# Value tiles copied by an engine where they keep their partitions, turned tiles copied by VectorE, and late loads moved behind the weights

## The chip, the cores and the metric

The kernel runs on one core of a Trainium2 chip. The metric is device time in microseconds of one execution. A core has five engines with a queue of instructions each, worked off in order: TensorE (PE; its weight loads are listed apart, as PEld), VectorE (DVE), ScalarE (ACT), GpSimd (POOL) and SyncE (SP). SP only issues DMAs here; GpSimd also issues some.

## The reference

Two branches run over the same x (2048 rows of 576) and are mixed by a gate per row.

```python
def _A_ref(x, mem0, Wq, Wk, Wv, Wo, seg_len):       # 32 heads of 128, 8 memory rows, segments of 32
    mask = (idx[:, None] < M) | (idx[:, None] >= idx[None, :])
    for s in range(n_seg):                          # 64 segments, one after the other
        h = concatenate([mem, x[:, 32*s:32*s+32]])  # 40 rows
        q, k, v = h @ Wq, h @ Wk, h @ Wv            # 576 -> 32 x 128 each
        p = softmax(where(mask, q k^T * scale, -1e9))
        o = (p v) @ Wo
        mem = o[:, :8]                              # feeds the next segment
        outs.append(o[:, 8:])
def _B_ref(x, wqkv, wo):                            # full attention, 32 heads of 18, 2048 x 2048
    ...
g = sigmoid((x * gate_w).sum(-1))
return g * a + (1 - g) * b
```

Branch A is a recurrence: a segment can't start before the memory rows of the one before are known. Branch B has no such order and is used to fill the time between A's steps.

## The kernel before, in words

**A planner writes the order.** Every piece of work is an `Op` with the engines that may do it, an assumed duration on each, the pieces that it needs and a priority from the table `RANK`. `Plan.run` (L104) places them one by one on simulated engines: `choose` (L197) takes, for each engine, the piece that can start first, then the one of the lowest priority number. Tokens stand for buffers and PSUM banks: a piece that takes one waits until another gives it back. SP's transfers get an assumed landing time (`transfer`, L65). The instructions of each engine are then emitted in this order. If TensorE would stand still in the plan while an accumulator of branch B is open, a filler matmul on zeros is inserted ("warm"; L767 in the column form of four matmuls, L773 in the full form of one).

**Start (some 120 us).** x is turned and projected to branch B's q, k and v, which are stored to DRAM (L622 to L664). At the same time GpSimd issues the loads of A's weights (L537, L542: four pieces each of wv, wq, wk), each one behind a mark that VectorE writes. `carrier(n, far)` names the queue of a load: SP, or GpSimd where `far` is true. Key chunks (`load_k`, L716) go to GpSimd from chunk 3 on, value chunks (`load_v`, L745) from chunk 4, query chunks (`load_q`) from chunk 2.

**Branch B's visits.** 512 visits: four row-tiled matmuls for scores (L795), one ScalarE exponential over 128x2048 (L804), four column-tiled matmuls with the values (L813). `ahead` and `behind` in `RANK` spread them over the segments.

**Branch A's segment.** The 40 rows are 32 rows computed in the recurrence (8 memory rows and 24 of x) and 8 rows of x that are projected beforehand, which are put in later. The 32 rows are projected in six blocks Q0, K0, Q1, K1, V0, V1 (L1120, 20 matmuls each; four column groups of the array hold four groups of heads). Each block is evicted from PSUM by VectorE or ScalarE into a tile `tm` of 128x512 (L412 or L410), of which there are four. Q and K tiles are turned by a DMA transpose (L1178, on SP) into `tt`, and copied into the tile `qk` (L1187) by VectorE or GpSimd. A V tile holds its rows in four blocks of 32 partitions; they have to be in `v_sb` at partitions 0 to 31 and 64 to 95, so four DMAs of SP carry each V tile there:

```python
for j in range(4):
    o = hf * 1024 + (j % 2) * 512
    dma(out=opened["v_sb"][64 * (j // 2):64 * (j // 2) + CT, o:o + 512], in_=tm[32 * j:32 * j + CT, :])
```

Blocks 0 and 2 keep their partitions in this, blocks 1 and 3 move down by 32. Then, for each half `hf` of the heads: scores (`psh`, L1203), exponential (L1213, ScalarE), masking by a minimum (`mn`, L1219, VectorE), sums (`pss`, L1229), reciprocal (L1238, VectorE), its broadcast (`prb`, L1246), the product (`nm`, L1256, VectorE), the product with v (`pso`, L1267), its eviction into `ot` (`co`, L412 or L410) and the output projection (`acc`, L1034). The memory rows are folded back (L1314) into the next segment's input. `pso` needs the transfers of v and the normalised weights. GpSimd also copies x columns into the next input (L1071 to L1073), the early projected rows into `qk` (L1089) and rows of `ot` aside (L1366).

SP's queue in a segment is: four transposes, eight v transfers, the early projected rows of a later segment, two loads of the early projected v rows (L1098).

Of the kernel before, what the change touches and what calls it, by code (L numbers as in the profile page):

```python
# [14 lines left out]


RANK = {
    "switch": 0.563, "near": 0, "early": 0.353, "wait": 0.266, "Q0": 0.487, "K0": 1.599, "Q1": 3.227,
    "K1": 2.483, "V0": 3.547, "V1": 5.796, "t0": 1.149, "t1": 0.73, "ph0": 6.746, "ph1": 0.999, "sm0": 1.555,
    "sm1": 0.05, "bc0": 0.05, "bc1": 1.126, "po0": 0.191, "po1": 0.05, "op0": 7.959, "op1": 0.124,  # L20
    "fo": 0.288, "lo0": 6.529, "lo1": 1.982, "la": 3.0, "ob": 0.777, "eQ": 5.514, "eK": 1.557, "eV": 0.427,
    "co": 0.869, "le": 4.086, "xp": 8.668, "mn": 0.05, "ct": 2.895, "fin": 16.977, "la_gate": 1, "lo_gate": 1,
    "ahead": 56, "behind": 1, "tail": 0.458, "gap": 0, "cool": 12.71,
}


# [18 lines left out]
class Plan:  # L45
# [56 lines left out]
        return end + self.DRAIN[dep.eng]  # L102

    def run(self):  # L104
        free = {e: 0.0 for e in ("PE", "DVE", "ACT", "POOL", "SP")}
        waiting = {e: [] for e in free}
        mode = None
        for op in self.ops:
            op.left = len(op.deps)
            for d in op.deps:  # L110
                d.users.append(op)
        for op in self.ops:
            if op.left == 0:
                for e in op.engs:
                    waiting[e].append(op)
        order = []
        n = len(self.ops)
        extra = 0
        open_ = False
        recent = []  # L120
        best = {}
        dirty = set(free)
        while len(order) < n + extra:
            for e in dirty:
                best[e] = self.choose(e, waiting[e], free[e], mode)
            pick = None
            for e in free:
                b = best[e]
                if b is not None and (pick is None or b[0] < best[pick][0]):
                    pick = e  # L130
            if pick is None:
                stuck = [(o.name, o.take) for e in free for o in waiting[e]]
                raise RuntimeError(f"nothing can be placed: {stuck[:20]}")
            est, op = best[pick]
            if pick == "PE" and open_ and self.warm is not None:
                for m in ("col", "full"):
                    if m not in (mode, op.mode):
                        continue
                    turn = 0.0 if mode == m else self.SWITCH
                    done = sum(d for t, d in recent if t > free["PE"] - 2.5)  # L140
                    if est - free["PE"] < self.WARM + turn + RANK["gap"] or done > RANK["cool"]:
                        continue
                    w = Op("warm", "PE", self.WARM, self.warm[m], [], 9.0, m, (), (), 0.0)
                    w.dmas, w.kb, w.slots, w.left = 0, 0.0, {}, 0
                    w.eng, w.start, w.end = "PE", free["PE"], free["PE"] + self.WARM + turn
                    free["PE"], mode = w.end, m
                    recent.append((w.end, self.WARM))
                    order.append(w)
                    extra += 1
                    pick = None  # L150
                    break
                if pick is None:
                    dirty = {"PE"}
                    continue
            waiting_engs = op.engs
            for e in waiting_engs:
                waiting[e].remove(op)
            dirty = set(waiting_engs)
            dirty.add(pick)
            dur = op.dur[op.engs.index(pick)]  # L160
            op.eng, op.start = pick, est
            if pick == "PE":
                if op.mode != mode:
                    dur += self.SWITCH
                mode = op.mode
                if op in self.opens:
                    open_ = True
                if op in self.closes:
                    open_ = False
                recent = recent[-8:]  # L170
                recent.append((est, dur * self.ARRAY[mode]))
            op.end = est + dur
            free[pick] = op.end
            if op.dmas and pick == "POOL":
                op.tail = 2.2 + op.kb / 250.0
            elif op.dmas:
                self.transfer(op)
                dirty.add("SP")
            for t in op.take:
                held = self.tokens[t]  # L180
                got = max(x for x in held if x[0] <= est + 1e-9)
                held.remove(got)
                op.slots.setdefault(t, []).append(got[1])
                dirty |= set(free)
            for t, taker, k in op.give:
                self.tokens[t].append((op.end + op.tail + self.DRAIN[pick], taker.slots[t][k]))
                dirty |= set(free)
            order.append(op)
            for u in op.users:
                u.left -= 1  # L190
                if u.left == 0:
                    for e in u.engs:
                        waiting[e].append(u)
                        dirty.add(e)
        return order

    def choose(self, e, ops, now, mode):  # L197
        found = []
        for op in ops:
            est = now  # L200
            for d in op.deps:
                a = self.after(d, e)
                if a > est:
                    est = a
            if op.dmas and e != "POOL":
                step = op.dur[op.engs.index(e)] / op.dmas
                for j in range(min(op.dmas, self.LANES)):
                    est = max(est, self.lanes[j] - j * step)
            blocked = False
            for t in set(op.take):  # L210
                k = op.take.count(t)
                held = sorted(self.tokens[t])
                if len(held) < k:
                    blocked = True
                    break
                if held[k - 1][0] > est:
                    est = held[k - 1][0]
            if not blocked:
                found.append((est, op))
        if not found:  # L220
# [32 lines left out]
def kernel(  # L253
# [475 lines left out]
    def load_k(c):  # L729
        g, kc = divmod(c, NQC)  # L730
        use = visits.get(("kuse", c - NKR))


        def fn(e):
            by_head(ktd, g, slice(kc * QC, (kc + 1) * QC), kring[c % NKR], False, queue(e))

        k_of[c] = add(f"lk{c}", *carrier(4, c >= 3), fn, [use, z_k[c % NKR], *stores_for(1, g, [kc])], prio=0.6, dmas=4, kb=90)

    def load_v(c):
        g, kc = divmod(c, NQC)  # L740
# [7 lines left out]
            )  # L748

        deps = [v_stores[hf * NKB + kb] for kb in range(4 * kc, 4 * kc + 4)]  # L750
        v_of[c] = add(f"lv{c}", *carrier(1, c >= 4), fn, [use, *deps], prio=0.65, dmas=1, kb=128)

    def load_q(i):
        g, qc = divmod(i, NQC)
        use = visits.get(("quse", i - NQR))

        def fn(e):
            by_head(qtd, g, slice(qc * QC, (qc + 1) * QC), qring[i % NQR], False, queue(e))

        q_of[i] = add(f"lq{i}", *carrier(4, i >= 2), fn, [use, z_q[i % NQR], *stores_for(0, g, [qc])], prio=0.55, dmas=4, kb=90)  # L760

    fin_state = {}
    last_vi = last_va = None
# [288 lines left out]
    for s in range(n_seg):  # L1052
# [100 lines left out]

        def put_v(hf, s=s):
            def fn(e):
                tm = box["tm", s, 2, hf]
                for j in range(4):
                    o = hf * 1024 + (j % 2) * 512
                    dma(  # L1159
                        out=opened["v_sb"][64 * (j // 2):64 * (j // 2) + CT, o:o + 512],  # L1160
                        in_=tm[32 * j:32 * j + CT, :],
                    )
            return fn

        pv0 = add(f"qv0.{s}", "SP", 2.5, put_v(0), [ev0, prev.get("pso0")], prio=0.2, give=(("tm", ev0, 0),), dmas=4, kb=128)
        pv1 = add(f"qv1.{s}", "SP", 2.5, put_v(1), [ev1, prev.get("pso1")], prio=0.2, give=(("tm", ev1, 0),), dmas=4, kb=128)

        acc_state = {}
        ots = []
        mids = {}  # L1170
        for hf in range(2):
            eq, ek, pvx = ((eq0, ek0, pv0), (eq1, ek1, pv1))[hf]

            turned = []
            for a, ev_a in ((0, eq), (1, ek)):
# [9 lines left out]
                def ct(e, hf=hf, s=s, a=a):  # L1185
# [4 lines left out]
                    )  # L1190

                turned.append(add(
                    f"ct{a}{hf}.{s}", ("DVE", "POOL"), (0.36, 0.85), ct, [t_, prev.get(f"psh{hf}")],
                    prio=RANK["ct"], give=(("tt", t_, 0),),
                ))

# [73 lines left out]
                            rhs=et[rr, r * L:(r + 1) * L], start=True, stop=True, tile_position=(64 * jj, 0),  # L1270
                        )

            o_ = add(f"po{hf}.{s}", "PE", 0.34, pso, [n_, lv, pvx], prio=RANK[f"po{hf}"], mode="tall", take=("pb", "pb"))
            cur[f"pso{hf}"] = o_
            for jj in range(2):
                def co(e, hf=hf, s=s, jj=jj):
# [269 lines left out]
```

## Time and profile before

| | |
|---|---|
| time, median of 3 runs | 1522.55 us (1519.33 to 1526.65) |
| span of the profiled execution | 1514.9 us |
| TensorE busy | 1404.0 us, 93% |
| ScalarE busy | 1051.5 us, 69% |
| VectorE busy | 753.8 us, 50% |
| GpSimd busy | 574.6 us, 38% |
| exponential of a visit, L804 | 512 of 1877 ns |
| eviction of a block by VectorE, L412 tm | 382 of 691 ns |
| turned copy, L1187 | 197 on VectorE of 323 ns, 59 on GpSimd of 625 ns |
| v transfers, L1159 | 512 on SP, 32 KB each |
| folds, L1314 | first at 178.6 us, sixteenth at 492.1 us: 20.9 us for a segment |

A line of a group of instructions names the line of code, the engine, the operation, output and input; then how many, their busy time and mean, and how long the engine stood idle ahead of them with what ended that. In an answer on waits a line has the engine, the line that waited, what released it, the total in us, how often and the longest. In a timeline a line has start and duration in us, and in brackets the idle time before it. "issue" stands for time in which the engine waited for nothing that the profile shows.

### The profile page before, as it was taken

The page shows a single profiled execution, that of the slowest core. Times are in us where ns is not written, and L with a number is a line of the kernel's source. Part 1 is how long each engine was busy: PE and PEld are TensorE (multiplying, and loading weights), DVE is VectorE, ACT ScalarE, POOL GpSimd, SP SyncE. Part 2 cuts the span into 40 slices and gives each one's busy share as a digit, 9 for nine tenths or more (in the row PEclk, how much of TensorE's full clock was granted, in tenths as well). Part 3 has the DMA queues.
Part 4 walks back from the last instruction along what each step waited for, and adds up shares of the span by engine and source line. Part 5 has one row for each costly group of instructions (what it writes and reads, how often), then busy time and mean ns, then how long its engine had stood idle before and what let it go on. Part 6 is the DMA issues. An engine that isn't in the chain of part 4 may idle for free.

```text
span 1514.9 us, 69086 instructions
## 1 busy us (share of the span) xinstructions
PE 1404.0 (93%) x30585; PEld 767.0 (51%) x30585; DVE 753.8 (50%) x1735; ACT 1051.5 (69%) x765; POOL 574.6 (38%) x1207
## 2 busy tenths in 40 slices
PE   6789899999999999999999999999999999999997
PEld 4346445555555545554555544555555455454545
DVE  6345454554555544555545554545554444444445
ACT  2125677777778777777778777767777777777770
POOL 6322125433352425343453325333453324333235
PEclk9799999999999999999999999999999999999999
DMA  8776633423333324333334333333334333333234
GB/s 277 225 276 187 132 67 80 84 63 70 68 79 71 67 64 86 73 67 69 72 83 66 68 68 83 72 59 70 79 81 84 60 60 74 60 61 60 51 108 132
DMA packets 355690, 138.52 MB, mean 91 GB/s; under 512 B 301095, under 2 KB 341431, under 8 KB 355391
## 3 DMA queue, kind: packets, MB, share of 16 engines
q1 hardware_dynamic: 327023, 89.55, 28.2%
q0 software_dynamic: 27216, 43.38, 10.0%
q8 instruction: 239, 3.92, 1.1%
q10 hardware_dynamic: 1152, 1.18, 0.3%
q14 instruction: 60, 0.49, 0.1%
HBM read 52.74 MB, written 30.86 MB: 55 GB/s over the span
## 4 chain that ended last, share of the span: by engine, by line
PE 63%; DMA 13%; ACT 12%; SPq 4%; issue 3%; DVE 3%; POOL 2%; ACTq 0%; DVEq 0%; POOLq 0%
PE pvv L1120 25%; ACT etb L804 11%; PE sb L795 10%; PE acc L1034 8%; PE ob L813 7%; DMA v_sb<-tm 5%; SPq L1159 3%; PE pv L894 3%; DMA tt<-tm 2%; PE pq L602 2%; PE ob L767 2%; PE pv L890 2%; DMA vgd<-vt 2%; PE psh L1203 1%; PE pso L1267 1%
## 5 line engine op out<-in xcount | busy, mean ns | idle before, releaser
L804 ACT ACTIVATE etb<-sb 128x2048 bf16<-128x2048 f32 x512 | 961.0, 1877 | 356.0 <-PE sb L795 334.7
L412 DVE CAST tm<-pvv 128x512 bf16<-128x512 f32 x382 | 263.7, 691 | 297.9 <-PE pvv L1120 297.1
L1120 PEld LDWEIGHTS <-ht 128*32 128x32 bf16 x7680 | 204.7, 97 | 187.3 <-DVE ht L1322 11.5
L795 PE MATMUL sb<-qch,kch 32*128 32x512 bf16 x2048 | 205.2, 388 | 33.4 <-ACT etb L804 23.6
L813 PE MATMUL ob<-etb,vch 128*32 128x512 bf16 x2048 | 206.2, 393 | 0.1
L1034 PE MATMUL acc<-wo,ot 128*32 128x144 bf16 x8192 | 161.6, 228 | 10.0 <-issue 9.3
L1034 PEld LDWEIGHTS <-ot 128*32 128x32 bf16 x8192 | 137.2, 98 | 29.9 <-issue 16.7
L1187 POOL COPY qk<-tt 128x512 bf16<-128x512 bf16 x59 | 36.8, 625 | 279.2 <-DMA tt<-tm 279.1
L795 PEld LDWEIGHTS <-kch 32*128 32x128 bf16 x2048 | 65.8, 91 | 151.1 <-issue 124.9
L1120 PE MATMUL pvv<-wq_m,ht 128*32 128x512 bf16 x2048 | 139.6, 380 | 0.3 <-issue 0.3
L1120 PE MATMUL pvv<-wv_m,ht 128*32 128x512 bf16 x2048 | 138.5, 379 | 0.0
L1120 PE MATMUL pvv<-wk_m,ht 128*32 128x512 bf16 x2048 | 135.3, 379 | 0.1
L412 DVE CAST ot<-pso 128x320 bf16<-128x320 f32 x179 | 83.4, 484 | 87.2 <-PE pso L1267 86.9
L813 PEld LDWEIGHTS <-vch 128*32 128x32 bf16 x2048 | 53.0, 93 | 106.6 <-issue 105.2
L1187 DVE COPY qk<-tt 128x512 bf16<-128x512 bf16 x197 | 63.6, 323 | 36.3 <-DMA tt<-tm 35.6
L1089 POOL COPY qk<-xl 128x256 bf16<-128x256 bf16 x128 | 50.4, 403 | 81.2 <-PE psh L1203 70.4
L1071 POOL COPY ht<-xg 128x96 bf16<-128x96 bf16 x64 | 17.1, 267 | 168.4 <-PE pvv L1120 149.7
L716 POOL DMA_DIRECT2D qch<-qtd x120 | 61.0, 515 | 42.6 <-PE sb L795 39.0
L1366 POOL COPY otl<-ot 128x256 bf16<-128x256 bf16 x64 | 25.7, 401 | 135.3 <-DVE ot L412 86.2
L1256 DVE TENSOR_TENSOR et<-et,prb 128x320 bf16<-128x320 bf16 x128 | 61.3, 479 | 31.6 <-PE prb L1246 30.4
L716 POOL DMA_DIRECT2D kch<-ktd x116 | 58.9, 514 | 45.1 <-PE sb L795 22.2
L716 POOL DMA_DIRECT2D otd<-stage x124 | 62.3, 509 | 36.0 <-DVE stage L856 34.9
(148 smaller groups left out, 1892.2 us busy)
## 6 DMA issues: line engine op xcount, KB each, us to landing
v_sb<-tm SPq DMA_DIRECT2D x512, 32.0 KB
xl<-qkd SPq DMA_DIRECT2D x64, 128.0 KB
qkd<-vl POOLq DMA_DIRECT2D x48, 128.0 KB, 2.6
wo<-in_A_Wo_dram POOLq DMA_DIRECT2D x4, 1152.0 KB, 8.4
vgd<-vt SPq DMA_DIRECT2D x32, 128.0 KB
wv_m<-in_A_Wv_dram POOLq DMA_DIRECT2D x4, 1024.0 KB, 8.5
wq_m<-in_A_Wq_dram POOLq DMA_DIRECT2D x4, 1024.0 KB, 10.1
wk_m<-in_A_Wk_dram POOLq DMA_DIRECT2D x4, 1024.0 KB, 8.7
```

The source lines that it names most:

```text
L412: nc.vector.tensor_copy(out=out_of(), in_=in_of())
L716: dma(out=rows_, in_=pads) if out else dma(out=pads, in_=rows_)
L795: nc.tensor.matmul(sb[:, j, :], lhsT=kc[r, o:o + P], rhs=qt_[r, :], start=True, stop=True, tile_position=(32 * j, 0),)
L804: nc.scalar.activation(out=etb[:, :, :], in_=box["sb", gq, kb][:, :, :], func=ACT.Exp, scale=scale_b)
L813: nc.tensor.matmul(ob[32 * j:32 * j + 32, :], lhsT=vc[:, o + 32 * j:o + 32 * j + 32], rhs=etb[:, j, :], start=(kb == 0), stop=(kb == NKB - ...
L894: nc.tensor.matmul(pv[:, k * P:(k + 1) * P], lhsT=lw, rhs=xL[:, cc, cols], start=(c == 0), stop=(c == NF))
L1034: nc.tensor.matmul(acc[32 * j:32 * j + 32, :], lhsT=o[:, slot, t0:t0 + CT], rhs=wo[:, h, RW * j:RW * j + RW], start=(first and s_ == 0), s ...
L1089: nc.gpsimd.tensor_copy(out=opened["qk"][:, f, :, 0:16 * L].rearrange("p a (h t) -> p a h t", t=L)[:, :, :, CT:L], in_=box["xlt", s][:, :, ...
L1120: nc.tensor.matmul(pv[32 * j:32 * j + 32, :], lhsT=ht[:, cc, :], rhs=rw, start=(c == 0), stop=(c == NF), tile_position=(0, 32 * j), skip_g ...
L1159: dma(out=opened["v_sb"][64 * (j // 2):64 * (j // 2) + CT, o:o + 512], in_=tm[32 * j:32 * j + CT, :],)
L1187: eng.tensor_copy(out=opened["qk"][:, hf, a, 0:16 * L].rearrange("p (j i t) -> p j i t", i=4, t=L)[:, :, :, 0:CT], in_=box["tt", s, a, hf] ...
L1256: nc.vector.tensor_tensor(out=et[:, :], in0=et[:, :], in1=box["prb", s, hf][:, :], op=ALU.mult)
```

## The change

Four things change in the code, and the table of priorities with them.

- A V tile's blocks 1 and 3 still go by DMA (two issues instead of four), blocks 0 and 2 are copied by VectorE or GpSimd, as the planner chooses. `pso` needs both, and the V tile is held until `pso` rather than until the transfers.
- The turned tiles are copied by VectorE only.
- Key chunk 3 is loaded by SP. The key and value chunks from 4 on and the query chunks from 2 on are planned after the last load of wk (the diff shows it for `load_k`; `load_v` and `load_q` get the same entry). This orders them in GpSimd's queue; in the built program they get no wait for that weight.
- `choose` gets a test on pieces that may run on several engines, and after each placement all engines choose anew.

```diff
-    "ahead": 56, "behind": 1, "tail": 0.458, "gap": 0, "cool": 12.71,
+    "ahead": 62, "behind": 0, "tail": 0.404, "qc": 2.731, "gap": 0, "cool": 7.325,
 ...
+            dirty |= set(free)
...
+            if not blocked and len(op.engs) > 1:
+                mine = est + op.dur[op.engs.index(e)]
+                for o, d in zip(op.engs, op.dur):
+                    if o != e and max([self.free[o]] + [self.after(x, o) for x in op.deps]) + d < -1.0:
+                        blocked = True
...
-        k_of[c] = add(f"lk{c}", *carrier(4, c >= 3), fn, [use, z_k[c % NKR], *stores_for(1, g, [kc])], ...)
+        k_of[c] = add(f"lk{c}", *carrier(4, c >= 4), fn, [use, z_k[c % NKR], *stores_for(1, g, [kc]), weight_loads["wk"][-1] if c >= 4 else None], ...)
 ...
...
         def put_v(hf, s=s):
             def fn(e):
+                move = nc.vector.tensor_copy if e == "DVE" else nc.gpsimd.tensor_copy if e == "POOL" else dma
                 tm = box["tm", s, 2, hf]
-                for j in range(4):
+                for j in (1, 3) if e == "SP" else (0, 2):
                     o = hf * 1024 + (j % 2) * 512
-                    dma(
+                    move(
...
-        pv0 = add(f"qv0.{s}", "SP", 2.5, put_v(0), [ev0, prev.get("pso0")], prio=0.2, give=(("tm", ev0, 0),), dmas=4, kb=128)
-        pv1 = add(f"qv1.{s}", "SP", 2.5, put_v(1), [ev1, prev.get("pso1")], prio=0.2, give=(("tm", ev1, 0),), dmas=4, kb=128)
+        for hf, ev in ((0, ev0), (1, ev1)):
+            before = [ev, prev.get(f"pso{hf}")]
+            pvs.append((
+                add(f"qv{hf}.{s}", "SP", 1.25, put_v(hf), before, prio=0.2, dmas=2, kb=64),
+                add(f"qc{hf}.{s}", ("DVE", "POOL"), (0.45, 1.1), put_v(hf), before, prio=RANK["qc"]),
+            ))
...
-                    f"ct{a}{hf}.{s}", ("DVE", "POOL"), (0.36, 0.85), ct, [t_, prev.get(f"psh{hf}")],
+                    f"ct{a}{hf}.{s}", "DVE", 0.3, ct, [t_, prev.get(f"psh{hf}")],
...
-            o_ = add(f"po{hf}.{s}", "PE", 0.34, pso, [n_, lv, pvx], ...)
+            o_ = add(f"po{hf}.{s}", "PE", 0.34, pso, [n_, lv, *pvx], ..., give=(("tm", evx, 0),))
```

## The prediction

> **What bounds the kernel now.** I read the page's chain first, then the waits of TensorE and of its weight loader with the start and the end cut away, then one segment in the timelines of SP, the weight loader and VectorE.
>
> ```profile
> PE 1404.0 (93%) x30585; PEld 767.0 (51%) x30585; DVE 753.8 (50%) x1735; ACT 1051.5 (69%) x765; POOL 574.6 (38%) x1207
> ...
> PE pvv L1120 25%; ACT etb L804 11%; PE sb L795 10%; PE acc L1034 8%; PE ob L813 7%; DMA v_sb<-tm 5%; SPq L1159 3%; PE pv L894 3%; DMA tt<-tm 2%; PE pq L602 2%; PE ob L767 2%; PE pv L890 2%; DMA vgd<-vt 2%; PE psh L1203 1%; PE pso L1267 1%
> ```
>
> TensorE is busy 93%, so its order of work, with the gaps in it, is the time. The chain passes through the copies into v_sb for 5% + 3%, about 120 us, but TensorE does other work beside most of that. What can be won is only where it stands still. Waits of TensorE from 180 to 1480 us:
>
> ```profile
> PE sb L795 <- ACT etb L804: 21.0, 59, 1.0
> PE pso L1267 <- DMA v_sb<-tm: 19.3, 25, 1.6
> PE acc L1034 <- issue: 10.0, 18, 0.9
> ```
>
> The same for its weight loader, in which a wait shows even while the last matmul drains:
>
> ```profile
> PEld L1267 <- DMA v_sb<-tm: 22.9, 30, 1.7
> ...
> PEld L1229 <- DVE et L1219: 13.4, 36, 0.5
> ...
> PEld L1246 <- DVE rq L1238: 11.4, 27, 0.4
> ...
> PEld L1203 <- POOL qk L1187: 6.1, 12, 0.8
> ```
>
> So v costs about 20 us, in 25 to 30 of the 128 half segments. The masking minimum (L1219) and the reciprocal (L1238) on VectorE already end 63 short waits: VectorE has little room there. One segment in three timelines (SP with all engines; weight loader; VectorE):
>
> ```profile
> 711.84 4.97 SPq L1159 DMA_DIRECT2D v_sb<-tm  x8
> 719.83 0.33 PEld L1267 LDWEIGHTS <-v_sb 64*128 64x128 bf16 x15 [1.25 <-DMA v_sb<-tm]
> ...
> 712.12 0.69 DVE L412 CAST tm<-pvv 128x512 bf16<-128x512 f32 x1 [1.07 <-PE pvv L1120]
> 712.73 0.45 DVE L1187 COPY qk<-tt 128x512 bf16<-128x512 bf16 x1
> 713.09 0.31 DVE L1219 TENSOR_TENSOR et<-et,cap 128x320 bf16<-128x320 bf16 x1
> 713.33 0.28 DVE L1187 COPY qk<-tt 128x512 bf16<-128x512 bf16 x1
> ```
>
> Eight issues follow each other at about 0.63 us; the last ended near 715.6, landed 4.2 us later, and the matmul at L1267 stood 1.25 us.
>
> **What the skill says.** "VectorE: DVE Perf Modes", section on the TRN2 errata, prices an SBUF to SBUF copy at 58 + FD/Accel cycles at 0.96 GHz (194 ns for 512 bf16 at four a cycle) and adds that the measured fixed part is nearer 150 cycles, from which I estimate 290 ns. The trace has 251/290/567 ns (min/median/max) for the turned copy, also 512 bf16 per partition, so I use 290. "SBUF — State Buffer", section "Who interferes with whom", says that such a fast copy and a GpSimd instruction exclude each other for a whole instruction. The trace agrees: the copy at 712.73 took 0.45 us beside GpSimd's copies (GpSimd was busy with L1073 and L1089 from 712.37 to 713.03), the one at 713.33 took 0.28. "DMA: Bandwidth & Descriptors", section on the anatomy of one DMA, gives about 2 us of fixed cost; here the last v transfer took 4.2 us in one segment and under 2 in another (issued to 1253.15, matmul at 1255.10), so its queueing is more than the price.
>
> **Part by part.** I compared the order in which the two built programs issue on each engine. TensorE's order hardly moves (segments 0 to 42 are the same but for single steps); what differs is counted below, against the span of 1514.9 us.
>
> 1. *v by VectorE or GpSimd.* SP's v issues fall from 512 to 256. New are 117 pairs of 32x512 copies on VectorE and 11 on GpSimd. SP issues 4 instead of 8 after the turns: 4 x 0.63 = 2.5 us off its queue, so the last transfer starts up to 2.5 us sooner. The longest wait is 1.7 us. The later half of v is evicted at 712.81, and its two issues can end by 714.3; with the same 4.2 us they land at 718.5, just when TensorE came there (718.49). I take 18 of the 20 us; bounds 10 (queueing stays) and 23. v tiles are held until L1267's matmul instead of the transfer; four buffers, and the next segment's first eviction comes after that matmul, so nothing.
>
> 2. *What these copies push.* A pair is 2 x 0.29 = 0.58 us and stands in VectorE's queue before the first half's masking minimum in most segments; behind it stand the reciprocal, the normalising product and the ot copies, for all of which TensorE waits. The first half's v pair fits in the 1.07 us idle before the eviction at 712.12. Of the second pair about 0.28 us disappears into the idle before the minimum (13.8 us in 49 times) or takes the place of a turned copy that now follows. Some 0.30 remains, and TensorE is already waiting there in about half of the segments: 0.17 x 64 = 11 us lost. Bounds: 0, and 0.58 x 64 = 37. The trace of before has no 32-partition copy, hence the range.
>
> 3. *Turned copies on VectorE only.* 59 leave GpSimd (625 ns) for VectorE (323 ns). 12 waits of 6.1 us on GpSimd's copies go, some come back on VectorE: gain 4, bounds 0 and 7. GpSimd's own waits for these transposes (279 us) were its spare time; its copies of x columns behind them wait for TensorE anyway.
>
> 4. *Replanned engines and fillers.* Filler work on TensorE falls from 239 to 198 column fillers and rises from 71 to 85 full ones; five column fillers in one piece last 1.25 us, the last ends 0.39 after its start, so each takes 0.215: (41 - 14) x 0.22 = 6 us less. It is a gap that the planner no longer sees, apart from the waits on v that it never saw. Of the ot copies 37 leave ScalarE (-37 x 0.424), and 22 tm and 10 vl evictions come (+22 x 0.586 + 10 x 0.583): +3 us busy, but in the attention stage, where ScalarE ends TensorE's 59 waits (21.0 us), it has half as many copies. I take 5 of the 21; bounds 0 and 10.
>
> 5. *Far loads behind the weights.* GpSimd's queue stood still before two of these loads:
>
> ```profile
> 40.22 2.03 POOL L716 DMA_DIRECT2D kch<-ktd  x4 [8.37 <-DMA ktd<-stg]
> 69.92 0.51 POOL L716 DMA_DIRECT2D kch<-ktd  x1 [11.85 <-DMA ktd<-stg]
> ```
>
> Up to eight weight loads were queued behind them; these loads now go to SP (one) or behind the last of wk, so weights start up to 20 us sooner. But the first 120 us move 251 GB/s, the last two wk loads stay behind the opening memsets (101 us) and the x columns (125 us), and the key and query pieces moved back are first used by visits 64 and 32, while 27 visits precede the first fold. TensorE's waits from 40 to 94 us are for evictions blocked by the stores of v (about 12 us), which share the DMA engines with the weights. I take a gain of 3; bounds a gain of 12 and a loss of 8. The extra test in the planner's choice compares a time that is never negative with -1, so it does nothing; the change of the dirty set shows only in the order.
>
> Sum: -18 + 11 - 4 - 6 - 5 - 3 = -25 us, span 1490. The three timed runs have a median of 1522.55, 7.7 above this span; the difference is carried over: 1497.5 us.
>
> **Rivals.**
> - *VectorE becomes the bound of the recurrence; slower.* Place: the v pair before L1219. If GpSimd's copies at that moment (0.40 us at L1089) also block the pair, the push is 0.58 + 0.40 = 0.98 us a segment, 63 us, against 36 of gains: +27, 1549. It decides from 36/64 = 0.56 us a segment; a lock in part of the segments, 0.75, gives +12, 1534. For it: VectorE's 63 short waits and the 0.45 us copy. Against: VectorE is at 50% and goes to 55% (117 x 0.58 + 59 x 0.32 + 37 x 0.484 - 22 x 0.69 - 10 x 0.69 = +83 us), and GpSimd loses 59 copies.
> - *A new wait takes the place of the old; no change.* Half of v still goes by DMA behind four transposes: if the wait falls by 10 only, and the push costs 0.4 x 64 = 26, the sum is -10 + 26 - 18 = -2, about 1520.
> - *More than thought.* The start loses the 12 us of blocked evictions instead of 3 and the push costs nothing: -25 - 9 - 11 = -45, 1477. For it: eight weight loads were held up by 22 us in all.
>
> **How the numbers follow.** The likeliest case has 0.62, its own range 1484 to 1511; more than thought 0.12, no change 0.14, slower 0.12. Half a per cent is 7.6 us, about what a measurement of this kernel can tell from no change. Faster: 0.62 + 0.12 + 0.02 of the edge of no change = 0.76; within: 0.13; slower: 0.11. The range reaches from 1479 to 1521: it leaves out half of the best case and nearly all of the slower one.
>
> **What the profile after would show.** Step 1: waits of L1267's successor for v under 5 us, SP's last v issue some 2.5 us sooner. Step 2: v_sb copies near 290 ns; waits of pss on the minimum up from 13.4 to some 20 to 25 us. Step 3: no GpSimd copy from tt. Step 4: waits of sb on etb near 16. Step 5: the first fold near 175 us instead of 178.6. I am wrong if v's copies last over 450 ns, if the wait for v stays above 10 us, or if the start moves by more than 10 us.

## The result and the profile after

The changed kernel takes 1499.94 us (median of 4 runs, 1495.88 to 1505.4) against 1520.94 us for the kernel before (4 runs beside them, 1515.47 to 1526.65): ratio 0.9864, 95% interval 0.9814 to 0.9913. The prediction was 1497.5 us. The medians differ by 21.0 us; the two profiled executions differ by less, 1514.9 against 1499.2 us, which is 15.7 us.

From the page of the kernel after: busy times, the chain by line, and two groups of copies.

```profile
PE 1388.5 (93%) x30405; PEld 763.4 (51%) x30435; DVE 833.4 (56%) x2033; ACT 1053.4 (70%) x760; POOL 553.2 (37%) x1166
...
PE pvv L1126 24%; ACT etb L810 13%; PE sb L801 11%; PE acc L1040 8%; PE ob L819 7%; DMA tt<-tm 6%; PE pv L900 4%; PE pq L608 2%; PE psh L1215 2%; DVE tm L418 2%; PE pv L896 2%; PE ob L773 1%; PE pso L1279 1%; DMA vgd<-vt 1%; PE prb L1258 1%
...
L1199 DVE COPY qk<-tt 128x512 bf16<-128x512 bf16 x256 | 76.7, 306 | 43.1 <-DMA tt<-tm 40.7
L1166 DVE COPY v_sb<-tm 32x512 bf16<-32x512 bf16 x234 | 70.5, 301 | 6.1 <-ACT tm L416 0.3
```

The v transfers and SP's issues of them, 5% + 3% of the chain before, are gone from it. In their place stand more of the exponential (13%) and of the transposes (6%). VectorE is busy 79.6 us more (the prediction had 83) and is still idle 44% of the time.

The waits of TensorE, 180 to 1480 us, kernel after:

```profile
PE sb L801 <- ACT etb L810: 18.3, 58, 0.6
PE pss L1241 <- DVE et L1231: 10.5, 15, 1.7
...
PE psh L1215 <- DVE qk L1199: 3.9, 9, 1.4
```

And of its weight loader:

```profile
PEld L1241 <- DVE et L1231: 21.9, 32, 2.0
...
PEld L1279 <- DMA v_sb<-tm: 3.4, 12, 0.8
```

The wait for v, 22.9 us at the loader before, is 3.4; the wait for the masking minimum (L1231 now), 13.4 before, is 21.9. The loader's wait is not TensorE's loss, since matmuls may still run during it. What TensorE itself lost shows in the groups of its matmuls, over the whole run. The kernel before, then the kernel after; between the bars stand the group's busy time and the mean of one matmul, behind the second bar how long TensorE stood idle ahead of the group:

```profile
L1267 PE MATMUL pso<-et,v_sb 64*128 64x40 bf16 x2048 | 55.8, 179 | 20.4 <-DMA v_sb<-tm 19.7
...
L1203 PE MATMUL psh<-qk 128*64 128x40 bf16 x2048 | 55.4, 189 | 7.1 <-POOL qk L1089 3.9 <-DVE qk L1187 2.0 <-POOL qk L1187 0.9
...
L1229 PE MATMUL pss<-bsel,et 128*128 128x2 bf16 x384 | 28.4, 166 | 0.8 <-DVE et L1219 0.7
```

```profile
L1215 PE MATMUL psh<-qk 128*64 128x40 bf16 x2048 | 55.4, 188 | 12.1 <-DVE qk L1199 4.7 <-POOL qk L1095 2.6 <-POOL ht L1078 1.3
...
L1279 PE MATMUL pso<-et,v_sb 64*128 64x40 bf16 x2048 | 48.2, 179 | 2.9 <-DMA v_sb<-tm 1.0 <-DVE ot L418 0.6 <-issue 0.5
...
L1241 PE MATMUL pss<-bsel,et 128*128 128x2 bf16 x384 | 28.8, 168 | 11.5 <-DVE et L1231 10.5
```

The product with v (`pso`) takes 25.1 us less, 17.5 of it idle time and 7.6 busy time. Against this TensorE stands 5.0 us more ahead of the scores (`psh`) and 10.7 us more ahead of the sums (`pss`, behind the minimum). The fillers are busy 11.0 us less (96.2 against 85.2 for both forms).

The segment that the prediction showed, in three timelines of the kernel after (SP; VectorE; weight loader):

```profile
706.20 3.44 SPq L1166 DMA_DIRECT2D v_sb<-tm  x4
...
707.04 0.69 DVE L418 CAST tm<-pvv 128x512 bf16<-128x512 f32 x1
707.77 0.68 DVE L1166 COPY v_sb<-tm 32x512 bf16<-32x512 bf16 x2
708.48 0.32 DVE L1231 TENSOR_TENSOR et<-et,cap 128x320 bf16<-128x320 bf16 x1
...
713.58 0.27 PEld L1279 LDWEIGHTS <-v_sb 64*128 64x128 bf16 x16
```

SP's last v issue ends at 709.64, 1.9 us after the eviction of the second half (707.73). Before, it ended at 711.84 + 4.97 = 716.81, 4.0 us after the eviction's end at 712.81. So it comes 2.1 us sooner, and the load of v at 713.58 waits for nothing. The pair of copies at 707.77 puts the minimum off to 708.48. In this segment that is without cost, as the weight loader comes to the sums at 708.86 and doesn't wait; in others it is the price.

Where the 15.7 us arose, by the times of the folds into the next segment's input (L1314 before, L1327 after):

| stretch | before | after | difference |
|---|---|---|---|
| start to the first fold | 178.6 | 180.3 | +1.7 |
| first to 16th fold | 313.5 | 310.0 | -3.5 |
| to the 35th | 396.0 | 392.4 | -3.6 |
| to the 55th | 409.1 | 401.3 | -7.8 |
| to the last | 161.2 | 159.3 | -1.9 |
| the rest | 56.5 | 55.9 | -0.6 |

The gain is spread over the recurrence, and the start gave none.

### The profile page after: what moved, and what is told of

Same layout as the page of the kernel before. It is cut to its first block, busy times and chain, and to the rows that moved or that the text cites. A ratio compares the mean times of both kernels' runs of the same rounds, so it can differ in the third digit from the quotient of the medians.

```text
span 1499.2 us, 68540 instructions
## 1 busy us (share of the span) xinstructions
PE 1388.5 (93%) x30405; PEld 763.4 (51%) x30435; DVE 833.4 (56%) x2033; ACT 1053.4 (70%) x760; POOL 553.2 (37%) x1166
## 3 DMA queue, kind: packets, MB, share of 16 engines
q0 software_dynamic: 27088, 43.31, 10.7%
## 4 chain that ended last, share of the span: by engine, by line
PE 66%; ACT 13%; DMA 10%; DVE 6%; issue 3%; POOL 1%; SPq 0%; ACTq 0%; DVEq 0%
PE pvv L1126 24%; ACT etb L810 13%; PE sb L801 11%; PE acc L1040 8%; PE ob L819 7%; DMA tt<-tm 6%; PE pv L900 4%; PE pq L608 2%; PE psh L1215 2%; DVE tm L418 2%; PE pv L896 2%; PE ob L773 1%; PE pso L1279 1%; DMA vgd<-vt 1%; PE prb L1258 1%
## 5 line engine op out<-in xcount | busy, mean ns | idle before, releaser
L418 DVE CAST tm<-pvv 128x512 bf16<-128x512 f32 x360 | 248.3, 691 | 256.8 <-PE pvv L1126 250.0
L418 DVE CAST ot<-pso 128x320 bf16<-128x320 f32 x216 | 98.6, 482 | 54.7 <-PE pso L1279 54.3
L1199 DVE COPY qk<-tt 128x512 bf16<-128x512 bf16 x256 | 76.7, 306 | 43.1 <-DMA tt<-tm 40.7
L1166 DVE COPY v_sb<-tm 32x512 bf16<-32x512 bf16 x234 | 70.5, 301 | 6.1 <-ACT tm L416 0.3
L1215 PEld LDWEIGHTS <-qk 128*64 128x64 bf16 x2048 | 45.0, 112 | 51.4 <-issue 38.8
```

The costliest lines, as they stand in the source:

```text
L418: nc.vector.tensor_copy(out=out_of(), in_=in_of())
L1166: move(out=opened["v_sb"][64 * (j // 2):64 * (j // 2) + CT, o:o + 512], in_=tm[32 * j:32 * j + CT, :],)
L1199: eng.tensor_copy(out=opened["qk"][:, hf, a, 0:16 * L].rearrange("p (j i t) -> p j i t", i=4, t=L)[:, :, :, 0:CT], in_=box["tt", s, a, hf] ...
L1215: nc.tensor.matmul(ph[64 * jj:64 * jj + 64, r * L:(r + 1) * L], lhsT=qk[:, hf, 1, k * L:k * L + 64], rhs=qk[:, hf, 0, k * L:(k + 1) * L], ...
```

## The experiments

All were timed beside runs of the kernel before. Ratios are to that kernel, with the 95% interval; one per cent is 15 us. Where two kernels of the experiments are compared, it is by these ratios. The main theory was the prediction's: fewer transfers end the wait for v, the copies give part of it back ahead of the minimum, and the priorities, the turned copies and the far loads add something. The rivals: the gain comes from the priorities or the start and not from v; or the copies cost nothing; or it is GpSimd's lock on VectorE that makes them dear.

**The transfers alone.** In the kernel before, only blocks 1 and 3 are transferred:

```diff
-                for j in range(4):
+                for j in (1, 3):
```

> The kernel before with blocks 0 and 2 of every V tile left out altogether: SP issues two transfers for a V tile instead of four, nothing copies the rest (so half of v stays zero), and the order planned is that of before on every engine. It shows what shorter v transfers are worth without the copies' cost. Main theory: TensorE's wait for v (19.3 us from 180 to 1480 us, 22.9 us at the weight loader) goes to under 5 us, the time falls by 16 to 22 us, ratio to before 0.986 to 0.990. Rival (the gain of the change lies in the new priorities and fillers): the wait is replaced by other waits and the time falls by under 8 us, ratio over 0.995.

Measured: 1493.66 us, 0.9834 (0.9796 to 0.9872), about 25 us. Weight loader, 180 to 1480 us:

```profile
PEld L1229 <- DVE et L1219: 14.3, 37, 0.8
...
PEld L1267 <- DMA v_sb<-tm: 1.4, 5, 0.4
```

The minimum is where it was (13.4 before), and the wait on v fell from 22.9 to 1.4 us. Halving the issues is enough to end the wait. The gain is larger than the wait that the lists show, and the group of the product has the rest:

```profile
L1267 PE MATMUL pso<-et,v_sb 64*128 64x40 bf16 x2048 | 47.8, 179 | 0.6 <-issue 0.4
```

TensorE stands 19.8 us less ahead of it (20.4 to 0.6), and the group is also busy 8.0 us less (55.8 to 47.8) with as many matmuls. Two products of the kernel before, the first without a wait for v and the second with one:

```profile
1252.38 0.37 PE L1267 MATMUL pso<-et,v_sb 64*128 64x40 bf16 x16
...
1254.31 0.19 PE L1267 MATMUL pso<-et,v_sb 64*128 64x40 bf16 x1
...
1255.10 0.46 PE L1267 MATMUL pso<-et,v_sb 64*128 64x40 bf16 x15 [0.61 <-DMA v_sb<-tm]
```

A product that waits is split: its first matmul runs alone, and the sixteen take 0.65 us of busy time instead of 0.37. Times the loader's 30 waits this is an estimate of 8 us, as the group shows.

**The v part alone.** The change of `put_v`, `pvs` and `pso` in the kernel before; old priorities (with `"qc": 2.731`), turned copies on both engines, far loads as before.

> The kernel before with the v part of the change alone (blocks 0 and 2 by VectorE or GpSimd, V tile held until the product with v); old priorities, turned copies on both engines, far loads as before. Main theory: -18 us for the wait, +10 for the pushed masking minimum, a few us for fillers and ScalarE: 10 to 18 us faster, ratio 0.988 to 0.993. Rival (priorities and fillers make the gain): under 6 us, ratio over 0.996.

Measured: 1508.85 us, 0.9929 (0.990 to 0.9958). Against the transfers alone, the copies give back 0.95%, some 14 us (about 7 to 22 us by the two intervals). Weight loader, 180 to 1480 us:

```profile
PEld L1235 <- DVE et L1225: 22.4, 60, 1.3
```

The wait on the minimum (L1225 here) is up from 14.3 us; ahead of the sums TensorE itself stands 8.0 us, against 1.3 with the transfers alone.

**All but the v part.** The kernel after, with v carried by four transfers:

```diff
-                for j in (1, 3) if e == "SP" else (0, 2):
-                    move(
+                for j in range(4):
+                    dma(
...
-            o_ = add(f"po{hf}.{s}", "PE", 0.34, pso, [n_, lv, *pvx], ...)
+            o_ = add(f"po{hf}.{s}", "PE", 0.34, pso, [n_, lv, pvx], ...)
```

> The changed kernel with v moved by four DMAs again; new priorities, turned copies on VectorE alone, far loads behind the weights. Main theory: without the v part nearly nothing is left: within 6 us of before, ratio 0.996 to 1.004, and TensorE waits for v some 20 us again. Rival (priorities, turned copies or loads make the gain): 10 us or more faster than before, ratio under 0.993.

Measured: 1520.58 us, 1.0006 (0.9989 to 1.0023): nothing. TensorE's waits, 180 to 1480 us:

```profile
PE pso L1273 <- DMA v_sb<-tm: 20.9, 28, 1.7
```

The wait for v is back (19.3 before). The profiled execution was the longest of the 22 (1533.49 us), so of its trace only this wait is used. Priorities, turned copies and far loads are worth nothing without the relief of v.

**No copies.** The kernel after, without the copies of blocks 0 and 2; the planned order of the rest stays:

```diff
-                for j in (1, 3) if e == "SP" else (0, 2):
+                for j in (1, 3) if e == "SP" else ():
```

> The changed kernel with the copies of blocks 0 and 2 left out (half of v stays zero), the planned order kept: it shows what the copies cost on VectorE and GpSimd. Main theory: the waits of pss on the minimum fall from 21.9 us at the weight loader back to some 12, and the time is 8 to 14 us below the changed kernel, some 1488 us, ratio to before 0.977 to 0.982. Rival (the copies fit in VectorE's idle time): within 4 us of the changed kernel, ratio to before about 0.986.

Measured: 1484.18 us, 0.9774 (0.9743 to 0.9804), 14 us below the kernel after. The wait on the minimum at the weight loader falls from 21.9 by 13.6:

```profile
PEld L1241 <- DVE et L1231: 8.3, 16, 1.9
```

This is a second value for the price of the copies, with the new priorities, and it equals the first. The price is not paid at the minimum alone, though the loader's list looks so. TensorE's groups here:

```profile
L1215 PE MATMUL psh<-qk 128*64 128x40 bf16 x2048 | 55.3, 189 | 5.1 <-POOL qk L1095 2.4 <-DVE qk L1199 1.8 <-POOL ht L1077 0.5
...
L1241 PE MATMUL pss<-bsel,et 128*128 128x2 bf16 x384 | 28.4, 166 | 3.7 <-DVE et L1231 3.1 <-DVE ot L418 0.3
```

Against the kernel after TensorE stands 7.8 us less ahead of the sums (11.5 to 3.7) and 7.0 us less ahead of the scores (12.1 to 5.1). Together this is about the 14 us.

**The copies twice.** The same line, with `(0, 2, 0, 2)`: 128 more pairs.

> The changed kernel with each pair of copies of V blocks executed twice in a row, in the same planned order. Main theory: the copies cost through the masking minimum behind them, about 14 us for the pairs there are (the run without copies against the changed kernel); with the idle ahead of them used up, the second pair of 0.58 us in front of the minimum costs 0.4 to 0.58 us in each of about 50 segments, so 20 to 35 us above the changed kernel, ratio to before 1.000 to 1.010. Rival (VectorE has room, the 14 us come from elsewhere, as from tiles held longer): under 8 us above the changed kernel, ratio under 0.992.

Measured: 1566.96 us, 1.0282 (1.0246 to 1.0318), some 64 us above the kernel after. This was far above what was expected. Weight loader, 180 to 1480 us:

```profile
PEld L1241 <- DVE et L1231: 59.5, 61, 2.4
PEld L1215 <- POOL ht L1079: 43.8, 35, 1.5
```

And VectorE in one segment:

```profile
598.58 1.23 DVE L1166 COPY v_sb<-tm 32x512 bf16<-32x512 bf16 x4
599.84 0.29 DVE L1199 COPY qk<-tt 128x512 bf16<-128x512 bf16 x1
...
600.77 1.31 DVE L1166 COPY v_sb<-tm 32x512 bf16<-32x512 bf16 x4
602.11 0.32 DVE L1231 TENSOR_TENSOR et<-et,cap 128x320 bf16<-128x320 bf16 x1
```

The first 128 pairs cost 14 us, 0.11 each; the second 128 some 64, 0.50 each, nearly their whole length (0.58). TensorE's idle time grows by 33.3 us ahead of the sums (11.5 to 44.8) and by 24.0 ahead of the scores (12.1 to 36.1). I read this as idle room on VectorE that the first pairs use up, so that what comes on top goes through to TensorE. In the segment shown the scores (L1215) come later by the doubled pair of the first half, which holds up the turned copy at 599.84 (it ends at 600.13, and TensorE loads at 600.25). The view names a GpSimd copy that ended at about the same moment, but the scores read the turned tile and not `ht`.

**The far loads.** The kernel after, with its far loads as in the kernel before:

```diff
-        k_of[c] = add(f"lk{c}", *carrier(4, c >= 4), fn, [use, ..., weight_loads["wk"][-1] if c >= 4 else None], ...)
+        k_of[c] = add(f"lk{c}", *carrier(4, c >= 3), fn, [use, ...], ...)
```

and the same for `load_v` and `load_q`.

> The changed kernel with the far loads where they were before (key chunk 3 on GpSimd, the later chunks not ordered behind the weights). Orders of the engines differ from the changed kernel's in GpSimd's start alone. Main theory, after the profile of the changed kernel (first fold at 180.3 us against 178.6 before): the start is set by the branch B projections and the DMAs, not by these loads, so the time is within 5 us of the changed kernel, ratio to before 0.983 to 0.990. Rival (the loads give several us that the start's other disturbances hide): 6 us or more above the changed kernel, ratio over 0.990.

Measured: 1499.26 us, 0.9843 (0.9815 to 0.9872), as the kernel after. TensorE's waits from 10 to 180 us in the kernel after:

```profile
PE sb L801 <- DMA kch<-ktd: 7.6, 1, 7.6
PE pvb L647 <- DVE wk_m L530: 3.7, 1, 3.7
```

and GpSimd's timeline there:

```profile
52.14 0.81 POOL L543 DMA_DIRECT2D wq_m<-in_A_Wq_dram  x1 [11.23 <-DVE wq_m L530]
61.79 0.81 POOL L543 DMA_DIRECT2D wq_m<-in_A_Wq_dram  x1 [7.88 <-DVE wq_m L530]
```

The weights no longer wait behind the far loads; they wait for VectorE's marks instead. GpSimd issues the last piece of wv at 35.83 us (45.83 before), but the first of wk at 78.17 (78.01 before) and the last at 129.30 (127.04 before), so the lead is lost on the way. And the first key chunk is waited for 7.6 us (2.9 before).

**Turned copies on both engines.** The kernel after, with `("DVE", "POOL"), (0.36, 0.85)` for the turned copies again.

> The changed kernel with the turned copies again on VectorE or GpSimd (the planner puts 83 of 256 on GpSimd). Main theory: a gain of 4 us was ascribed to VectorE alone; so 2 to 8 us above the changed kernel, ratio to before 0.988 to 0.992. Rival (VectorE is the tight engine now, so GpSimd's help is worth more than its slower copies cost): 3 us or more below the changed kernel, ratio under 0.984.

Measured: 1497.14 us, 0.9831 (0.9797 to 0.9864): not slower. This part brought nothing that can be measured. Ahead of the scores TensorE stands 7.2 us here and 12.1 us in the kernel after, so there the turned copies were not better off on VectorE alone.

**The priorities on top of the v part.** The kernel of the second experiment with the new table of priorities; turned copies, `choose` and far loads as before.

> The kernel before with the v part and the new priorities; turned copies on both engines and far loads as before. It differs from the run of the v part alone (ratio 0.993) in the table of priorities only, and from the changed kernel in the two parts that cost nothing when undone singly. Theory: the priorities fit the v part and bring the rest, ratio to before 0.983 to 0.988. Rival (priorities bring nothing, as they brought nothing without the v part; the two other parts do it only together, or the start of that run was slow by chance): ratio 0.990 to 0.995.

Measured: 1497.68 us, 0.987 (0.9847 to 0.9892), which is 9 us below the v part alone and equal to the whole change. So v and the priorities are all of it. How much of the 9 us the priorities themselves bring is less sure: in the profiles the first fold comes at 180.1 us here and at 185.1 in the v part alone, and kernels that are planned alike lie anywhere from 177.6 to 183.6. From the first fold to the last the two differ by 7.6 us (1256.8 against 1264.4), so most of it does lie in the recurrence. Fillers explain little of it: both forms together are busy 87.9 us here and 90.4 us in the v part alone.

**A later place for the second pair.** The kernel after, with VectorE's copies of the second half issued after the first half's reciprocal:

```diff
+                if e == "DVE" and hf == 1 and ("passed", s) not in box:
+                    box["late", s] = fn
+                    return
...
+                if hf == 0:
+                    box["passed", s] = True
+                    if ("late", s) in box:
+                        box.pop(("late", s))("DVE")
```

> The changed kernel in the same planned order on every engine, except that VectorE copies the second half's V blocks after the first half's reciprocal instead of ahead of its masking minimum, in the stretch in which it waits for TensorE's broadcast. Main theory: the same copies cost little there: the waits of pss on the minimum fall from 21.9 us to 12 to 15, the time is 5 to 10 us below the changed kernel, ratio to before 0.979 to 0.983. Rival (it is VectorE's total load that costs): within 3 us of the changed kernel, ratio about 0.986, and the waits only move to the products behind.

Measured: 1506.15 us, 0.9884 (0.9858 to 0.9911): not faster, and this expectation fell. The waits moved, as its rival had it. The minimum is freed, but the time isn't. Weight loader, then TensorE, 180 to 1480 us:

```profile
PEld L1244 <- DVE et L1234: 11.4, 19, 1.7
```

```profile
PE pv L900 <- DVE vl L418: 5.6, 9, 0.6
PE psh L1218 <- DVE qk L1202: 5.2, 11, 1.3
PE pss L1244 <- DVE et L1234: 4.3, 10, 1.2
PE pso L1286 <- DVE et L1275: 3.9, 11, 0.7
```

What now stands behind the pair in VectorE's queue (the eviction of the early v rows and the normalising product) is waited for instead. At TensorE: 4.8 us more for the early rows (L896 and L900 together 7.7, 2.9 in the kernel after), 1.3 for the scores, 3.4 for the product (0.5 to 3.9), 6.2 less for the minimum (10.5 to 4.3), and a first fold that is 1.7 us later (182.0). That is +5.0 of the 5.4 us between the two spans (1504.6 and 1499.2).

**Without GpSimd's pairs.** In the kernel after, 11 pairs run on GpSimd, all of the second half and late in the run. One of them, in timelines of VectorE and GpSimd:

```profile
1313.86 1.40 POOL L1166 COPY v_sb<-tm 32x512 bf16<-32x512 bf16 x2 [0.47 <-DVE tm L418]
...
1314.03 0.73 DVE L1231 TENSOR_TENSOR et<-et,cap 128x320 bf16<-128x320 bf16 x1
1314.69 0.71 DVE L1199 COPY qk<-tt 128x512 bf16<-128x512 bf16 x1
```

Beside it the minimum takes 0.73 instead of 0.32 us and the turned copy 0.71 instead of 0.29. The next kernel gives these pairs to VectorE:

```diff
-                move = nc.vector.tensor_copy if e == "DVE" else nc.gpsimd.tensor_copy if e == "POOL" else dma
+                move = dma if e == "SP" else nc.vector.tensor_copy
```

> The changed kernel in its planned order, with the 11 pairs of V blocks that GpSimd copies (segments 46 to 62) copied by VectorE at the place where GpSimd's stood. Main theory: in the changed kernel a GpSimd pair took 1.4 us and held up VectorE's masking minimum (0.73 instead of 0.32 us) and turned copy (0.71 instead of 0.29 us) at 1313.86 us, about 0.8 us; a VectorE pair costs up to 0.58. So 2 to 5 us below the changed kernel, ratio to before 0.981 to 0.985, waits of pss on the minimum after 1080 us down from 15.1 to about 10 us. Rival (no lock; VectorE's extra work costs): the same or 3 to 6 us above the changed kernel.

Measured: 1502.46 us, 0.9878 (0.9846 to 0.991): not faster; the expectation fell. From 1080 to 1450 us, where nearly all of the 11 pairs lie, the loader waits 14.5 us on the minimum, against 14.3 in the kernel after: giving the pairs to VectorE didn't shorten that wait. The 2 to 5 us that were expected of the time are not more than half the width of its interval, so a small effect either way would not show.

**All second pairs on GpSimd.**

```diff
-                move = nc.vector.tensor_copy if e == "DVE" else nc.gpsimd.tensor_copy if e == "POOL" else dma
+                move = dma if e == "SP" else nc.gpsimd.tensor_copy if hf else nc.vector.tensor_copy
```

> The changed kernel in its planned order, with the second half's V blocks copied by GpSimd in every segment. VectorE loses 53 pairs of 0.58 us. Main theory (a GpSimd copy of some 0.6 us holds up VectorE's copies and minima for its whole length): slower than the changed kernel by 10 to 30 us, ratio to before 0.99 to 1.005, minima and turned copies over 0.4 us on average. Rival (VectorE's queue alone costs): VectorE is relieved, the time falls by 5 to 10 us below the changed kernel, ratio about 0.98.

Measured: 1498.24 us, 0.9846 (0.982 to 0.9871), as fast as the kernel after: neither the loss that was expected of the lock nor the rival's gain. Groups of this kernel, and its weight loader's wait:

```profile
L1199 DVE COPY qk<-tt 128x512 bf16<-128x512 bf16 x256 | 96.1, 381 | 41.3 <-DMA tt<-tm 39.0
L1166 POOL COPY v_sb<-tm 32x512 bf16<-32x512 bf16 x128 | 80.6, 629 | 30.1 <-DVE tm L418 24.1
...
L1231 DVE TENSOR_TENSOR et<-et,cap 128x320 bf16<-128x320 bf16 x128 | 50.4, 394 | 23.7 <-ACT et L1225 23.3
```

```profile
PEld L1241 <- DVE et L1231: 14.5, 25, 1.5
```

The lock is there: the mean turned copy rises from 306 to 381 ns, the minimum from 351 to 394. But VectorE no longer spends 0.58 us on the pair itself, and the wait on the minimum falls from 21.9 to 14.5. The loss and the relief are of one size in the time.

**Copies for the first half only.** The second half goes by four transfers again, six in a segment:

```diff
-                for j in (1, 3) if e == "SP" else (0, 2):
+                for j in ((0, 1, 2, 3) if hf else (1, 3)) if e == "SP" else () if hf else (0, 2):
```

> The changed kernel in its planned order, with the second half's V tile moved by four DMAs again; only the first half's blocks 0 and 2 are copied, by VectorE. SP issues six v transfers in a segment. Main theory: the second half's pair is what pushes the minimum (it costs most of the 14 us), and two issues less are enough for most of the waits for v (mean 0.8 us, 1.25 us of issues saved): waits for v 3 to 8 us, pss on the minimum about 10 us, time 3 to 9 us below the changed kernel, ratio to before 0.980 to 0.984. Rival (the first half's pair costs as much, or six transfers are too many): at or above the changed kernel, ratio 0.986 to 0.992, waits for v over 12 us.

Measured: 1491.76 us, 0.9823 (0.980 to 0.9846), the fastest of those that carry all of v. Weight loader, 180 to 1480 us:

```profile
PEld L1241 <- DVE et L1231: 10.1, 18, 2.0
...
PEld L1279 <- DMA v_sb<-tm: 3.6, 12, 1.0
```

Six issues end the wait for v as well as four do (3.6 against 3.4 us), and the second half's pair was 11.8 of the 13.6 us by which copies lengthened the loader's wait on the minimum. But the first half's pair is not cheap for that. TensorE's groups:

```profile
L1215 PE MATMUL psh<-qk 128*64 128x40 bf16 x2048 | 55.4, 188 | 12.4 <-POOL qk L1095 3.5 <-DVE qk L1199 2.9 <-POOL ht L1078 2.1
...
L1241 PE MATMUL pss<-bsel,et 128*128 128x2 bf16 x384 | 28.5, 166 | 4.0 <-DVE et L1231 3.8
```

Ahead of the sums TensorE stands as long as without any copy (4.0 against 3.7 us), ahead of the scores as long as in the kernel after (12.4 against 12.1). So the second half's pair costs some 7.5 us ahead of the sums and the first half's some 7.3 ahead of the scores. The times agree: this kernel lies 0.49% (7 us) above the one without copies, and 0.41% (6 us) below the kernel after, though the intervals touch in the first case and overlap in the second. That the first pair holds up the scores through the turned copies behind it, as in the segment of the doubled copies, was read from that trace; the releasers named here are mixed.

## Why the prediction was right, step by step

The time was met within 2.4 us, and the mechanism in the main too: the wait for v ended, and part of the gain was given back by the copies. That it was met so closely is partly luck. The forecast added 7.7 us to its span of 1490, since the timed runs before lay that much above the profiled one; the span after came out at 1499.2, and the timed runs lie 0.7 above it. And errors of the steps cancel: steps 1 and 2 bring 11 us and not 7, steps 3 to 5 bring 9 and not 18. The parts of the runs sum to -20 us (-25 + 14 - 9), the medians differ by 21.0; the forecast's sum was -25:

| step | forecast | runs | from |
|---|---|---|---|
| 1, fewer transfers | -18 | -25 | transfers alone |
| 2, copies | +11 | +14 | transfers alone against v alone; no copies against the kernel after |
| 3, turned copies | -4 | 0 | on both engines again |
| 4, plan and fillers | -11 | -9 | priorities on top of v |
| 5, far loads, start | -3 | 0 | far loads as before |

- **Step 1** held and was somewhat small: the interval of the run gives 19 to 31 us. The loader's wait fell by 19.5 of 22.9 us. What it left out is that a product that waits for v is split, which costs some 8 us of busy time beside the wait. Of its working one number was misread: SP's last issue before ended at 716.81 us and not near 715.6, so the transfer took 3.0 us until the matmul at 719.83, not 4.2. The shift, forecast as 2.5 us, was 2.1.
- **Step 2** held in size, and in place for one half. It took the first half's pair to fit into VectorE's idle time; that pair costs TensorE some 7.3 us ahead of the scores, and the second half's some 7.5 behind the minimum instead of 11. The copy's median is 284 ns (forecast 290, which follows the fixed part of some 150 cycles that the Trainium skill's "VectorE: DVE Perf Modes" gives in its section on the TRN2 errata; its other value, 194 ns, is not seen here). The loader's wait on the minimum went to 21.9 us, inside the 20 to 25 forecast. The doubled copies show that the price is no constant: 0.11 us a pair now, 0.50 for the next.
- **Step 3** failed: the gain of 4 us is not found. The loader's waits of 6.1 us on GpSimd's copies went, but TensorE's on VectorE's turned copies rose from 2.0 to 3.9 us, and with both engines it stands less ahead of the scores (7.2 against 12.1 us).
- **Step 4**: fillers changed as counted (956 to 792 column matmuls, 71 to 85 full ones), but their busy time fell by 11.0 us and not 6. Waits on the exponential fell from 21.0 to 18.3 us, by 2.7 and not 5. The sum of 11 us agrees with the 9 us that the priorities bring on top of v, but not by its terms: between those two kernels the fillers differ by 2.5 us, and the waits on the exponential hardly (16.7 and 16.5 us). The run without the v part shows that the priorities are worth something only with it. Which of them does it was not tried.
- **Step 5** failed in sign, by little: the first fold came at 180.3, not 175. The far loads in themselves are worth nothing. It failed in what it took to hold up the weights: with the far loads out of the way, GpSimd waits for VectorE's marks (11.23 and 7.88 us). How the first fold varies by some us between kernels whose start should be alike (183.2 us with GpSimd's pairs on VectorE, 177.6 with all second pairs on GpSimd) is not explained.
- **The rivals.** The slower one needed 0.56 us lost in a segment; the copies cost 14 us in 64 segments, 0.22 us each. Doubled, they cost 78 us, 1.2 us each, and the kernel is slower than the kernel before (1.0282). It was right on the lock, which "SBUF — State Buffer" of the Trainium skill states in "Who interferes with whom" and the 0.73 us minimum shows, but it hardly meets the pairs: 11 of 128 run on GpSimd, and even all 64 pairs of the second half there cost no time on balance. "No change" fell with the 3.4 us wait for v; "more than thought" fell with the start.

Open: what the priorities change that is worth 9 us, why giving GpSimd's pairs to VectorE gained nothing, and what shares of the start's few us are chance. With the second pair after the reciprocal, the waits balance as counted above; that each of them follows from the moved pair was read from the traces and not tried by itself.

## What to carry to other kernels

When a wait is the tail of a queue of issues, take off as few of them as end it: here six transfers did as well as four. An instruction added to an in-order queue costs what is left of it after the idle time ahead of the operations that another engine waits for, so the price jumps once that idle time is used up (0.11 us a pair, then 0.50). Ask this of every such operation behind it and not of one: here the minimum, where the price was looked for, carried half of it, and the scores the other half. Moving the copies into a gap of VectorE's queue or to GpSimd moved the waits and brought no time. Read a loss from the idle and the busy time of the waiting group, since a list of waits missed 8 us of it here. And retune an order's priorities after the wait that they were fitted to is gone: here the new ones were worth 0.6% then, and nothing before.

## What the hardware showed that was not expected

- A copy of 32x512 lasts as long on VectorE as one of 128x512: means of 301 and 306 ns. On GpSimd it takes 629 ns (32x512) against 625 (128x512).
- A pair of GpSimd copies stretched two neighbours on VectorE by 0.4 us each in the segment shown (minimum 0.32 to 0.73, turned copy 0.29 to 0.71), and yet giving GpSimd all 64 pairs of the second half left the time where it was.
- An issue of v on SP took 589 ns (median) in the kernel before and 581 after, so the queue ahead of the last transfer weighed more than its landing: in the segment shown eight issues took 5.0 us, and the last transfer 3.0 until TensorE went on.
- Sixteen matmuls of a product that waits for v after the first took 0.65 us of busy time instead of 0.37; over the run the group is busy 55.8 us with eight transfers in a segment, 49.5 with six and 48.2 with four.
